# Attention with normalised queries and keys, then a feed-forward block: the first quad's squares split over two engines, and the work at the start of the last stage put in other places

## The chip, the cores and the metric

The kernel runs on one core of a Trainium2 chip. A core has engines with a queue of instructions each: TensorE (PE in the profile; its weight loads are listed as PEld), VectorE (DVE), ScalarE (ACT), GpSimd (POOL) and SyncE (SP), which issues nearly all of the kernel's transfers. An engine works through its queue in order, and waits where an instruction needs something that isn't there yet. The metric is the time of one execution on the device in microseconds (us). It covers a little more than the span, which is the time from the first to the last instruction of the profile.

## The reference

Two parts follow each other. Everything is float32; q, k and v have the shape (8, 12, 448, 64): 8 batches, 12 heads, 448 rows, 64 columns.

```python
q_n, k_n = (rmsnorm(q, g_q), rmsnorm(k, g_k))     # x / sqrt(mean(x * x) + 1e-06) * g
scores = scale * np.matmul(q_n, k_n.transpose(0, 1, 3, 2))
attn = np.exp(scores - max) / (sum + 1e-09)
attn_out = np.matmul(attn, v)
x = attn_out.transpose(0, 2, 1, 3).reshape(3584, 768)

h = x @ w_in                                      # 768 x 1024
e = np.exp(h - h_max)
solu = h * e / (np.sum(e) + 1e-09)
ln = (solu - mean) / np.sqrt(var + 1e-06) * g_ln
out = ln @ w_out                                  # 1024 x 768
```

## The kernel before

The work has three stages, all in the function `fast_path`, and PE goes from one to the next without a barrier.

**Attention.** A "pair" is two heads of one batch; a "quad" `m` is two pairs, `a = 2m` and `b = 2m + 1`. There are 24 quads. The program order of this stage is written out by hand: `tc.manual_schedule()` keeps each engine's instructions in the order in which the Python code issues them. For each pair the rows of q and k are squared (`squares`, one ACT instruction of 128x896, L662), summed over 32 columns (`row_sums`, a DVE reduction, L670), and, for the two pairs of a quad together, the two halves of a head are added by `fold_sums`: four POOL copies of 32 partitions (L680) and an addition (L681). `rsqrt_seed` takes the inverse root by Ln and Exp on ACT (L687, L688), `rsqrt_step` refines it by one Newton step of four small DVE instructions (L694 to L697), `normalise` multiplies q and k by it on POOL (L703), `qk_transpose` is a DVE transpose (L713), and `gain` multiplies by the gains on ACT (L717). Then `scores` multiplies keys by queries on PE in three blocks of keys (L802), `scores_last` does the last 64 keys of both pairs at once (L815), and each block is followed by its exponential E on ACT (L792). `add` adds two blocks of E on DVE (L829), `add_more` a third on POOL (L838), `values` and `values_last` multiply E by v, and `sums` gets the sums of E.

The first quad, m = 0, has a sequence of its own (from L1394), since nothing is ready ahead of it. Pairs 0 and 1 are loaded and normalised in another layout (`square_rows`, `normalise_rows` at L762, `transpose_rows` and `take_rows`), and between their scores the squares of pairs 2 and 3 (quad 1) and 4 and 5 (quad 2) are made, with `fold_sums(1)` and `fold_sums(2)`. The call `norms_next()` stands for the inverse root and the normalisation of the next quad. In this text the "fourth pair" is pair 3.

**The product with w_in.** 3584 tokens are 28 tiles `t` of 128; a group `g` of 14 holds tiles 2g and 2g + 1. A group's product is done in seven partial products (Strassen's scheme, `products`), which end with P4 and P3; the results are added up by DVE (L996), which also keeps the maximum of a row. When a tile's h is complete, `done` plans its five further steps: exponential (`ff_exp`, ACT, L1051), product (`ff_mult`, DVE, L1055), moments (`ff_moments`: two BNStats of 128x512 at L1063, small DVE instructions at L1064 to L1068, then a power and a product on POOL at L1069 and L1071), normalisation (`ff_norm`, ACT, L1075) and `ff_spread`, a DVE transpose (L1084) followed by four stores from SP (L1087) that write the tile to a buffer `ud` in DRAM. The steps are due a number of units after the tile is complete; a unit is one partial product in this stage, and four slots in the last. By default the units are (1, 2, 3, 5, 7); three of the last four tiles have their own (L1096 to L1098). Of a group the tile 2g + 1 is complete first, so tile 26 is the last one.

**The product with w_out.** The last stage has seven supersteps `n` of four tiles each (4n to 4n + 3). Both the four tiles together and each partial product inside are done with Strassen's scheme, seven outer products by seven inner ones. The outer ones run in the order P1, P5, P6, P2, P7, P3, P4, seven slots apart (`STEP`), and the inner ones of an outer product are put in slots 0, 4, 8, 10, 12, 16 and 20 from its start (`PLACES`), so three outer products overlap. A slot is one inner product, four matmuls of 128x192. Its results are copied from the PSUM banks A, B, C by ACT (L1206) or added by DVE (L1208, L1233, L1246, L1256); banks are reused, so a later group of matmuls waits until the reader is done. `both` (L1284) adds two results.

The operands of a superstep are called a11, s1, s2, a12, s3, s4, a22. `load_u` reads tiles from `ud` (SP, L1131); `make` forms the operands: a11, a12 and a22 are ACT copies (L1149, L1151, L1153), s1 is a DVE addition (L1155), s2, s3 and s4 are DVE subtractions (L1157, L1159, L1161), each in two halves `t` of 128x512. s2 is s1 minus a11, s3 is a11 minus a loaded tile, s4 is a12 minus s2. `inner_sums` makes four more sums of each operand on POOL (L1172 to L1175, 128x256 each). In which slot each half is made is set by `made(n, name, slot of half 0, slot of half 1)`; for superstep 0 the slots are its own (L1590 on), for the others they are set against the superstep before. The dictionary `at` maps slots to such calls, and after each slot's matmuls they are issued in order; due steps of `later` come with the matmuls of the slot.

Of the kernel before, what the change touches and what calls it, by code (L numbers as in the profile page):

```python
# [366 lines left out]
def fast_path(  # L367
# [274 lines left out]
    def load_v(m, queue=nc.sync):  # L642
# [13 lines left out]
                lasts[m + i] = vl[:, 2 * i : 2 * i + 2]  # L656
        d["vl"] = lasts.pop(m)

    def squares(n):
        d = st[n]  # L660
        d["sq"] = work.tile([P, 2 * NB, 32], FP32, tag="sq", name="sq", bufs=2)
        nc.scalar.activation(d["sq"].rearrange("p (s b) d -> p s (b d)", s=2), d["qk"], AF.Square)  # L662
# [429 lines left out]
    def in_parts():  # L1092
        def done(g, i):
            t = 2 * g + i
            ff_max(t)
            waits = {  # L1096
                (NG - 2, 1): (1, 2, 3, 5, 5), (NG - 1, 1): (1, 2, 3.25, 6.75, 7), (NG - 1, 0): (2.25, 3.75, 4.75, 7.5, 8)
            }.get((g, i), (1, 2, 3, 5, 7))  # L1098
            for x, f in zip(waits, (ff_exp, ff_mult, ff_moments, ff_norm, ff_spread)):
                later(x, lambda f=f: f(t))  # L1100

        p = [products(g, lambda i, g=g: done(g, i)) for g in range(NG)]
        parts = [p[0][1], p[0][2]]
        for g in range(NG):
            turn = [p[g][6], p[g][5], p[g][7], p[g][4], p[g][3]]
            x = len(parts)
            if g + 1 < NG:
                turn[3:] = [p[g + 1][1], p[g][4], p[g + 1][2], p[g][3]]
            parts += turn
            if g + 1 < NG:  # L1110
                follow(parts, x, lambda g=g: sizes(g + 1))
                follow(parts, x + 1, lambda g=g: block_sums(g + 1, 0))
                follow(parts, x + 2, lambda g=g: block_sums(g + 1, 1))
            if g + 2 < NG:
                follow(parts, x + 4, lambda g=g: load_x(g + 2))
        return parts
# [27 lines left out]
    def make(n, name, t):  # L1144


        o = operand(n, name)[:, t]
        if name == "a11":
            nc.scalar.copy(o, in_turn(n, t, 0))  # L1149
        elif name == "a12":  # L1150
            nc.scalar.copy(o, in_turn(n, t, 1))  # L1151
        elif name == "a22":
            nc.scalar.copy(o, in_turn(n, 2 + t, 1))  # L1153
        elif name == "s1":
            nc.vector.tensor_tensor(o, in_turn(n, 2 + t, 0), in_turn(n, 2 + t, 1), OP.add)  # L1155
        elif name == "s2":
            nc.vector.tensor_tensor(o, us[n, "s1"][:, t], us[n, "a11"][:, t], OP.subtract)  # L1157
        elif name == "s3":
            nc.vector.tensor_tensor(o, us[n, "a11"][:, t], in_turn(n, 2 + t, 0), OP.subtract)  # L1159
        else:  # L1160
            nc.vector.tensor_tensor(o, us[n, "a12"][:, t], us[n, "s2"][:, t], OP.subtract)  # L1161
# [144 lines left out]
    def unit(f, steps=4):  # L1306
        nonlocal now
        f()
        now += steps
        due = [x for x in todo if x[0] <= now]  # L1310
        todo[:] = [x for x in todo if x[0] > now]
        for _, g in sorted(due, key=lambda x: x[0]):
            g()
# [40 lines left out]
    with tc.manual_schedule():  # L1354
# [19 lines left out]
        for m in range(NQ):  # L1374
            a, b = 2 * m, 2 * m + 1

            def outputs():
                values_last(m)
                values(a)


            next1 = m + 1 < NQ
            next2 = m + 2 < NQ
            next3 = m + 3 < NQ
            early = m > 0 and next1

            def norms_next():
                rsqrt_seed(norms[m + 1])
                rsqrt_step(norms[m + 1])
                normalise(a + 2)  # L1390
                normalise(b + 2)

            if m == 0:
                unit(lambda: scores(a, 0))  # L1394
                normalise_rows(1, 0)
                normalise_rows(1, 1)
                unit(lambda: scores(a, 1))
                unit(lambda: scores(a, 2))
                for s in range(2):
                    transpose_rows(1, s)  # L1400
                    take_rows(1, s)
                squares(2)
                add(a)
                add_more(a)
                row_sums(2)
                unit(lambda: scores_last(m))
                squares(3)
                unit(lambda: scores(b, 0))
                row_sums(3)
                fold_sums(1)  # L1410
                unit(lambda: scores(b, 1))
                unit(lambda: scores(b, 2))
                add(b)
                norms_next()
                squares(4)
                row_sums(4)
                squares(5)
                unit(outputs)
                qk_transpose(2)
                gain(2)  # L1420
                row_sums(5)
                qk_transpose(3)
                fold_sums(2)
                unit(lambda: values(b))
                unit(lambda: sums(m))
                inverse(m)
                later(1, lambda m=m: divide(m))
                continue
            if early:
                norms_next()  # L1430
            for x in joins_at.get(m, ()):
                combine_in(x)
            if next1:
                load_v(m + 1)
            if m == 1:
                load(m + 3)
            unit(lambda: scores(a, 0))
            if m == 1:
                gain(3)
            store_x(m - 1)  # L1440
            if early:
                qk_transpose(a + 2)
                if next3 and m > 1:
                    load(m + 3)
            unit(lambda: scores(a, 1))
            unit(lambda: scores(a, 2))
            unit(lambda: scores_last(m))
            unit(lambda: scores(b, 0))
            unit(lambda: scores(b, 1))
            if early:  # L1450
                qk_transpose(b + 2)
            add(a)
            if not on_vector(m):
                add_more(a)
            unit(lambda: scores(b, 2))
            if next2:
                squares(a + 4)
                squares(b + 4)
                row_sums(a + 4)
            if next1:  # L1460
                gain(a + 2)
                gain(b + 2)
            if next2:
                row_sums(b + 4)
                fold_sums(m + 2)
            add(b)
            if on_vector(m):
                add_more(a)
                add_more(b)
            unit(outputs)  # L1470
            step(m - 2)
            begin(m)
            step(m - 1)
            if m - 1 in sets:
                load_next()
            if m == 2:
                load_next()
                load_next()
            if m == 3:
                norm_gain()  # L1480
            unit(lambda: values(b))
            if m == NQ - 1:
                block_sums(0, 0)
                block_sums(0, 1)
                load_x(1)
            unit(lambda: sums(m))
            inverse(m)
            if next1:
                later(1, lambda m=m: divide(m))
            if m == NQ - 2:  # L1490
                load_x(0)
                sizes(0)
# [54 lines left out]
        def when(slot, f):  # L1547
            at.setdefault(slot, []).append(f)
# [6 lines left out]
        for n in range(NS):  # L1555
            base = period * n
            for i, name in enumerate(ORDER):
                q = len(ORDER) * n + i
                for place, f in zip(PLACES, outer_product(n, name, q)):
                    assert STEP * q + place not in slots  # L1560
                    slots[STEP * q + place] = f
                x = HALVES[name][0]
                if q > 1:
                    when(STEP * q - 6, lambda n=n, x=x: inner_sums(n, x))
            for x, t, slot in (("V", 1, 31), ("V", 0, 34), ("C22", 1, 45), ("C22", 0, 52)):
                when(base + slot, lambda n=n, x=x, t=t: both(n, x, t))
            if n == 0:
# [3 lines left out]
            blocks = (0, 0), (1, 0), (2, 0), (3, 0), (2, 1), (3, 1), (0, 1), (1, 1)  # L1571
            for slot, (t, h) in zip(at_load, blocks):
                when(base + slot, lambda n=n, t=t, h=h: load_u(n, t, h))
            late = 6 if n == 1 else 0
            made(n, "a11", base + 12 + late, base + 15 + late)
            made(n, "s1", base + 21 + late, base + 24 + late)
            made(n, "s2", base + 28 + late, base + 38)
            made(n, "a12", base + 33, base + 36)
            made(n, "s3", base + 40, base + 42)
            made(n, "s4", base + 47, base + 49)  # L1580
            made(n, "a22", base + 53, base + 55)

        for h in range(2):
            for t in (2, 3):
# [2 lines left out]
            load_u(0, t, 1)  # L1587
        for x in ("s2", "a12", "s3", "s4", "a22"):
            operand(0, x)
        made(0, "s2", 0, 3)  # L1590
        made(0, "s3", 6, 8)
        made(0, "a12", 10, 11)
        made(0, "a22", 12, 14)
# [87 lines left out]
```

## Time and profile before

| What | us |
|---|---|
| runs of the kernel | 806.71, 807.04, 807.82 (median 807.04) |
| the profiled execution | 807.2 |
| its span | 805.4 |
| span from the start to the second quad's first scores | 26.0 |
| start of the last stage (first group of L1194) | 569.6 |

The granted clock of PE was 0.997 of full speed over the span. Two quantities of the profile have to be kept apart. An engine's busy time is the sum of its instructions; what an engine costs is the time that PE, which is nearly always busy, stands still for it. The profile gives this as the idle time ahead of an instruction, with the name of what it waited for in square brackets. The timeline lists an engine's instructions with start and length; lines with "x4" are four alike in a row. Of POOL's queue one sees at the handover from the second to the last stage that it has a long pause, here 9.41 us:

```profile
576.56 0.86 POOL L1069 TENSOR_TENSOR he<-he,mhalf 128x1 f32<-128x1 f32 x1 [9.41 <-ACT u L1206]
577.52 1.37 POOL L1071 TENSOR_SCALAR shift<-mv,he 128x1 f32<-128x1 f32 x1
578.84 0.73 POOL L1172 TENSOR_TENSOR sums<-s 128x256 f32<-128x256 f32 x1
```

The first start of the second line and the end of the line before show that instructions of one engine follow each other within some tenths of a microsecond if nothing holds them.

### The profile page before, as it was taken

What the parts mean: (1) busy time and instruction counts of PE and PEld (TensorE: products, weight loads), DVE (VectorE), ACT (ScalarE), POOL (GpSimd) and SP (SyncE); (2) the same over time, 40 slices, a digit from 0 to 9 for tenths busy, and PEclk for the clock granted to TensorE, in tenths of its full rate; (3) what the DMA queues carried; (4) which work ended last, traced back from release to release, by engine and by line L of the source; (5) the groups of instructions that cost most, each with busy time, mean ns of one, the idle gap of its engine ahead of it and who ended that gap; (6) DMA issues with size and microseconds to landing.
All of it is one profiled execution on the core that took longest, in us unless ns stands there. A gap on an engine that the chain in (4) does not pass through costs nothing.

```text
span 805.4 us, 14271 instructions
## 1 busy us (share of the span) xinstructions
PE 789.7 (98%) x4854; PEld 464.5 (58%) x4854; DVE 612.8 (76%) x1203; ACT 473.0 (59%) x783; POOL 519.9 (65%) x662
## 2 busy tenths in 40 slices
PE   8999999999999999999999999999899999999997
PEld 4344444443444433444444444444699999999996
DVE  6787989989888896488778667776886776866945
ACT  6677878878778764467767544453505455464420
POOL 2666777778777775244466466678487777777861
PEclk9999999999999999999999999999999999999999
DMA  9878899897787832555545445542647457366312
GB/s 170 159 168 156 182 194 184 196 187 161 165 160 169 161 103 66 140 131 151 150 131 147 102 119 140 141 110 52 210 125 252 133 188 267 117 229 213 120 60 83
DMA packets 269598, 122.68 MB, mean 152 GB/s; under 512 B 187596, under 2 KB 254668, under 8 KB 269516
## 3 DMA queue, kind: packets, MB, share of 16 engines
q1 hardware_dynamic: 254332, 111.78, 55.7%
q10 hardware_dynamic: 15184, 9.90, 4.5%
q8 instruction: 40, 0.66, 0.3%
q14 instruction: 42, 0.34, 0.1%
HBM read 84.94 MB, written 36.70 MB: 151 GB/s over the span
## 4 chain that ended last, share of the span: by engine, by line
PE 88%; DVE 3%; DMA 2%; SPq 2%; POOL 2%; ACT 1%; issue 1%; DVEq 0%; ACTq 0%; POOLq 0%
PE A L1194 15%; PE A L980 13%; PE o L859 12%; PE s L802 12%; PE B L980 8%; PE B L1194 8%; PE C L980 4%; PE sm L881 4%; PE D L980 4%; PE C L1194 4%; PE s L815 2%; PE o L848 2%; SPq L636 1%; DMA ur<-ud 1%; DMA xg<-xd 1%
## 5 line engine op out<-in xcount | busy, mean ns | idle before, releaser
L792 ACT ACTIVATE E<-s 128x896 f32<-128x896 f32 x168 | 138.8, 939 | 8.9 <-PE s L802 8.1
L802 PE MATMUL s<-qkT 64*64 64x448 f32 x1152 | 120.1, 545 | 1.7 <-ACT qkT L717 1.0
L859 PE MATMUL o<-E,v 128*64 128x448 f32 x576 | 113.8, 543 | 0.0
L1069 POOL TENSOR_TENSOR he<-he,mhalf 128x1 f32<-128x1 f32 x28 | 27.6, 986 | 105.6 <-DVE he L1068 95.7
L1194 PE MATMUL B<-w_out,sums 128*128 128x192 f32 x392 | 80.6, 329 | 3.3 <-DVE P L1256 2.1
L802 PEld LDWEIGHTS s<-qkT 64*64 64x64 f32 x1152 | 48.1, 163 | 60.0 <-ACT E L792 29.2
L1194 PE MATMUL A<-w_out,sums 128*128 128x192 f32 x392 | 80.6, 329 | 1.0 <-POOL sums L1175 0.7
L859 PEld LDWEIGHTS o<-E,v 128*64 128x64 f32 x576 | 39.1, 137 | 72.2 <-issue 68.0
L703 POOL TENSOR_TENSOR qkn<-qk,ny 128x896 f32<-128x896 f32 x46 | 77.1, 1697 | 3.5 <-DMA qk<-in_q_dram 1.5
L838 POOL TENSOR_TENSOR es<-es,E 128x896 f32<-128x896 f32 x22 | 46.4, 2109 | 48.9 <-ACT sq L662 35.4
L980 PE MATMUL B<-w_in,xsum 128*128 128x512 f32 x168 | 76.7, 593 | 0.5 <-POOL he L1069 0.5
L980 PE MATMUL A<-w_in,xg 128*128 128x512 f32 x168 | 74.6, 593 | 0.0
L1194 PEld LDWEIGHTS B<-w_out,sums 128*128 128x128 f32 x392 | 66.9, 191 | 3.9 <-DVE P L1256 2.4
L1051 ACT ACTIVATE u<-h,hmax 128x1024 f32<-128x1024 f32 x28 | 32.1, 1148 | 62.7 <-DVE hmax L1045 62.7
L1194 PEld LDWEIGHTS A<-w_out,sums 128*128 128x128 f32 x392 | 66.8, 191 | 1.7 <-POOL sums L1175 1.6
L980 PEld LDWEIGHTS B<-w_in,xsum 128*128 128x128 f32 x168 | 31.8, 190 | 41.0 <-issue 39.0
L980 PEld LDWEIGHTS A<-w_in,xg 128*128 128x128 f32 x168 | 31.8, 190 | 40.1 <-issue 39.3
L829 DVE TENSOR_TENSOR es<-E 128x896 f32<-128x896 f32 x48 | 53.0, 1107 | 2.1 <-ACT E L792 2.1
L670 DVE TENSOR_REDUCE part<-sq 128x28 f32<-128x896 f32 x46 | 47.9, 1080 | 4.4 <-ACT sq L662 2.0
L680 POOL COPY ss<-part 32x56 f32<-32x56 f32 x92 | 46.8, 508 | 6.7 <-DVE part L670 2.2
L713 DVE STREAM_TRANSPOSE qkT<-qkn 128x896 f32<-128x896 f32 x46 | 48.4, 1087 | 0.4 <-POOL qkn L703 0.4
L1194 PE MATMUL A<-w_out,s 128*128 128x192 f32 x224 | 45.6, 326 | 0.0
(150 smaller groups left out, 1647.8 us busy)
## 6 DMA issues: line engine op xcount, KB each, us to landing
ur<-ud SPq DMA_DIRECT2D x60, 256.0 KB, 4.7
ud<-ub SPq DMA_DIRECT2D x112, 128.0 KB, 2.3
xd<-xo SPq DMA_DIRECT2D x48, 224.0 KB, 3.0
qk<-in_q_dram SPq DMA_DIRECT2D x92, 112.0 KB, 3.2
qk<-in_k_dram SPq DMA_DIRECT2D x92, 112.0 KB, 3.0
v<-in_v_dram SPq DMA_DIRECT2D x24, 384.0 KB, 4.4
out_dram<-P SPq DMA_DIRECT2D x19, 384.0 KB, 4.3
raw<-in_moe_w_in_dram SPq DMA_DIRECT2D x12, 512.0 KB, 5.5
```

Of the source, the lines that this page charges most:

```text
L670: nc.vector.tensor_reduce(norms[m]["part"][:, i], st[n]["sq"], AX, OP.add)
L680: e.tensor_copy(ss[g * 32 : g * 32 + 32], part[o * 32 : o * 32 + 32])
L703: e.tensor_tensor(d["qkn"].rearrange("p (s b) d -> p s b d", s=2), d["qk"].rearrange("p s (b d) -> p s b d", d=32), y.rearrange("p (s b) - ...
L713: nc.vector.transpose(d["qkT"].rearrange("p s t -> p (s t)"), d["qkn"].rearrange("p b d -> p (b d)"))
L792: nc.scalar.activation(d["E", kc], s[:, :, 0:S], AF.Exp)
L802: nc.tensor.matmul(s[c : c + D, h, 0:S], d["qkT"][hh, 1, keys], d["qkT"][hh, 0, :], start=True, stop=True,)
L829: nc.vector.tensor_tensor(d["es"], d["E", 0], d["E", 1], OP.add)
L838: e.tensor_tensor(d["es"], d["es"], d["E", 2], OP.add)
L859: nc.tensor.matmul(d["o"][h * D : (h + 1) * D, :], quads[n // 2]["v"][:, n % 2 + 2 * h, kc], d["E", kc][:, h], start=False, stop=(kc == NJ ...
L881: nc.tensor.matmul(sm[g : g + 32, :], ones[:, w], e[:, h, t * S // 2 : (t + 1) * S // 2], start=(x == 0), stop=(x == len(terms) - 1),)
L980: nc.tensor.matmul(k[bank], a[:, c], w_in[i][:, c], start=begin and c == 0, stop=c == HD - 1, skip_group_check=not begin,)
L1194: nc.tensor.matmul(k[bank], a[:, c].rearrange("p a i -> p (a i)"), w_out[:, area, i, c], start=begin and c == 0, stop=c == KC - 1, skip_gr ...
```

## The change

In the first quad, the squares of the fourth pair are made in two halves: q's by DVE, ahead of the second pair's `transpose_rows`, and k's by ACT, behind `squares(2)`. `row_sums(3)` and `fold_sums(1)` come directly after `scores_last`, and the exponential of `scores(b, 2)` is issued behind `norms_next()`'s instructions. PE's order stays the same.

In the second stage the units after which the last tiles' steps are due are changed: tile 24 has its moments and normalisation one unit later; tile 27 its transpose a quarter; tile 26 its product half a unit, its moments two, its normalisation half a unit and its transpose three quarters. On DVE this puts one result of the last w_in group (L996) ahead of tile 24's moments, and tile 26's moments behind several results of the last stage.

In the last stage s2 of superstep 0 is made by POOL in slots 0 and 1 (DVE in slots 0 and 3 before), the inner sums of superstep 0's third outer product (s2) are issued at slot 5 (8 before), and s1, s2, s3, s4 and a22 of superstep 1 are made in later slots, from 39 to 57 (27 to 55 before). The other supersteps keep their slots.

```diff
+    def squares_half(n, s, vector):
+        d = st[n]
+        if s == 0:
+            d["sq"] = work.tile([P, 2 * NB, 32], FP32, tag="sq", name="sq", bufs=2)
+        y, x = d["sq"].rearrange("p (s b) d -> p s (b d)", s=2)[:, s], d["qk"][:, s]
+        if vector:
+            nc.vector.tensor_tensor(y, x, x, OP.mult)
+        else:
+            nc.scalar.activation(y, x, AF.Square)
...
             waits = {
-                (NG - 2, 1): (1, 2, 3, 5, 5), (NG - 1, 1): (1, 2, 3.25, 6.75, 7), (NG - 1, 0): (2.25, 3.75, 4.75, 7.5, 8)
+                (NG - 2, 1): (1, 2, 3, 5, 5), (NG - 2, 0): (1, 2, 4, 6, 7),
+                (NG - 1, 1): (1, 2, 3.25, 6.75, 7.25), (NG - 1, 0): (2.25, 4.25, 6.75, 8, 8.75),
             }.get((g, i), (1, 2, 3, 5, 7))
...
         elif name == "s2":
-            nc.vector.tensor_tensor(o, us[n, "s1"][:, t], us[n, "a11"][:, t], OP.subtract)
+            (nc.vector if n else nc.gpsimd).tensor_tensor(o, us[n, "s1"][:, t], us[n, "a11"][:, t], OP.subtract)
...
                 unit(lambda: scores(a, 2))
+                squares_half(3, 0, True)
                 for s in range(2):
                     transpose_rows(1, s)
                     take_rows(1, s)
                 squares(2)
+                squares_half(3, 1, False)
                 add(a)
                 add_more(a)
                 row_sums(2)
                 unit(lambda: scores_last(m))
-                squares(3)
-                unit(lambda: scores(b, 0))
                 row_sums(3)
                 fold_sums(1)
+                unit(lambda: scores(b, 0))
                 unit(lambda: scores(b, 1))
-                unit(lambda: scores(b, 2))
                 add(b)
                 norms_next()
+                unit(lambda: scores(b, 2))
                 squares(4)
...
                 if q > 1:
-                    when(STEP * q - 6, lambda n=n, x=x: inner_sums(n, x))
+                    when(STEP * q - 6 if q > 2 else 5, lambda n=n, x=x: inner_sums(n, x))
...
-            late = 6 if n == 1 else 0
-            made(n, "a11", base + 12 + late, base + 15 + late)
-            made(n, "s1", base + 21 + late, base + 24 + late)
-            made(n, "s2", base + 28 + late, base + 38)
+            late = n == 1
+            made(n, "a11", base + 12 + 6 * late, base + 15 + 6 * late)
+            made(n, "s1", base + 21 + 18 * late, base + 24 + 17 * late)
+            made(n, "s2", base + 28 + 15 * late, base + 38 + 7 * late)
             made(n, "a12", base + 33, base + 36)
-            made(n, "s3", base + 40, base + 42)
-            made(n, "s4", base + 47, base + 49)
-            made(n, "a22", base + 53, base + 55)
+            made(n, "s3", base + 40 + 7 * late, base + 42 + 7 * late)
+            made(n, "s4", base + 47 + 4 * late, base + 49 + 4 * late)
+            made(n, "a22", base + 53 + 2 * late, base + 55 + 2 * late)
...
-        made(0, "s2", 0, 3)
+        made(0, "s2", 0, 1)
```

## The prediction

> **What bounds the kernel now.** I read the page's busy line first, then the chain that ended last, then the waits of TensorE (PE), and only then the timelines around the two places that the diff touches.
>
> ```profile
> PE 789.7 (98%) x4854; PEld 464.5 (58%) x4854; DVE 612.8 (76%) x1203; ACT 473.0 (59%) x783; POOL 519.9 (65%) x662
> PE 88%; DVE 3%; DMA 2%; SPq 2%; POOL 2%; ACT 1%; issue 1%; DVEq 0%; ACTq 0%; POOLq 0%
> ```
>
> PE is busy for 789.7 of 805.4 us and carries 88% of the chain. The change touches no matmul, so it can win only from PE's 15.7 idle us and from stretches where PE's clock was low. The list of PE's waits says which idle time is large (columns: total, times, longest, us):
>
> ```profile
> PE B L1194 <- DVE P L1256: 2.1, 1, 2.1
> PE s L815 <- ACT E L792: 1.3, 2, 0.7
> PE s L802 <- ACT qkT L717: 1.0, 1, 1.0
> PE B L1194 <- DVE P L1246: 1.2, 1, 1.2
> PE A L1194 <- POOL sums L1175: 0.7, 1, 0.7
> PE B L980 <- POOL he L1069: 0.5, 1, 0.5
> ```
>
> PE's timeline places them; two lie in the second quad, four where the w_in stage hands over to the last stage:
>
> ```profile
> 26.02 2.60 PE L802 MATMUL s<-qkT 64*64 64x448 f32 x24 [1.03 <-ACT qkT L717]
> 29.28 1.53 PE L815 MATMUL s<-qkT 64*64 64x448 f32 x8 [0.66 <-ACT E L792]
> ...
> 566.92 2.81 PE L980 MATMUL B<-w_in,xsum 128*128 128x512 f32 x6 [0.52 <-POOL he L1069]
> ...
> 579.34 0.92 PE L1194 MATMUL B<-w_out,sums 128*128 128x192 f32 x4 [1.16 <-DVE P L1246]
> ...
> 584.35 0.92 PE L1194 MATMUL B<-w_out,sums 128*128 128x192 f32 x4 [2.15 <-DVE P L1256]
> ...
> 586.16 1.49 PE L1194 MATMUL A<-w_out,sums 128*128 128x192 f32 x4
> ...
> 597.47 0.89 PE L1194 MATMUL A<-w_out,sums 128*128 128x192 f32 x4 [0.66 <-POOL sums L1175]
> ```
>
> Start to start, undisturbed groups of four matmuls are 0.65 apart. Against that, 579.34 comes 1.32 late, 584.35 2.31 late, 597.47 0.82 late; 566.92 is 0.69 late against six-matmul groups of 2.58. The windows show why 585.10 to 588.72 took 3.62 us for three groups (1.67 too long): after the long idle time the granted clock (column PEclk) fell.
>
> ```profile
> 579.00:584.00 5.00, 2.87 (x16) 2.57 (x16) 4.83 (x14) 3.54 (x6) 4.58 (x8) 1.00 0.71 250
> 584.00:589.00 5.00, 4.65 (x18) 4.65 (x19) 2.85 (x9) 0.42 (x1) 4.92 (x7) 0.66 0.73 202
> ```
>
> With 0.38 of small change after the stalls, the handover loses 0.69 + 1.32 + 2.31 + 1.67 + 0.82 + 0.38 = 7.2 us. From 579 to 584 DVE is busy 4.83 of 5.00: it is the late engine there, and its timeline shows with what.
>
> ```profile
> 577.53 1.22 DVE L1055 TENSOR_TENSOR u<-h,u 128x1024 f32<-128x1024 f32 x1
> ...
> 578.93 0.35 DVE L1246 TENSOR_TENSOR P<-B,u 128x192 f32<-128x192 f32 x1
> ...
> 579.46 1.28 DVE L1063 BATCH_NORM_STATS2 bs<-u 128x6 f32<-128x512 f32 x2
> ...
> 582.82 1.23 DVE L1084 STREAM_TRANSPOSE ub<-u 128x1024 f32<-128x1024 f32 x1
> 583.98 0.31 DVE L1256 TENSOR_TENSOR P<-B,u 128x192 f32<-128x192 f32 x1
> ```
>
> PE's group at 584.35 needs the 0.31 us sum at 583.98; ahead of it in DVE's queue stand the moments and the transpose of the last token tiles.
>
> **The Trainium skill.** "PSUM — Partial Sum Buffer", section Engine vs sequencer instructions, says that the queues of ScalarE (ACT), VectorE (DVE) and GpSimd (POOL) are strictly first in, first out. The trace agrees: ACT's E at 28.33 stood behind the Ln at 27.80, which waited 1.83 for POOL. "SBUF — State Buffer", section Who interferes with whom, says that a DVE instruction with two SBUF inputs and a GpSimd instruction lock each other out of a shared port, whichever issues second. It agrees: of the four POOL copies from 18.73 (1.83 us together) one ran 1.04 and the others some 0.25, beside DVE's two-input add at 19.11; POOL's shift at 577.52 took 1.37 under DVE's L1055 and 0.26 elsewhere. I use this below.
>
> **First quad.** Removed: the 0.94 us ACT square of the fourth pair. Added: a DVE square of 128x448 and an ACT square of 128x448. Neither shape is in the trace; ACT's 128x896 at 0.94 and its 128x448 copies at 0.65 bound ACT's half between 0.47 and 0.67; DVE's 128x512 two-input ops ran 0.68, so 0.6. DVE's half costs nothing: it fits the 1.03 idle before DVE's copy at 13.93, from about 12.8 to 13.4; were it 0.5 longer, PE's third group of scores would be late by as much. ACT's half pushes E of scores_last from 15.71 to about 15.83, hidden since PE has scores until 17.5. row_sums(3) then ends at 17.55 instead of 18.59, and POOL (free at 17.81) starts the fold at 17.87 instead of 18.73. DVE's add(b), at 18.40, now runs into the third copy, as it did before: I take the end of the fold at 20.1 (19.25 without the collision, 20.22 with the worst) instead of 20.94. Behind it: Ln and Exp, Newton step, normalise, transpose, gain, so scores of the second quad could start by 0.85 earlier; PE is free at 25.0, so the 1.03 wait is nearly gone. But scores(b,2)'s E now stands behind Ln and Exp on ACT, and squares(4) behind it, which costs 0.36 of the lead for the second fold. The wait at 29.28 ends on that chain (fold, Ln, E): it moves from 29.28 to about 28.65. Gain 0.6, bounds 0.2 to 1.5; from there PE runs unbroken and carries the lead on.
>
> **Moments later.** The B sum of the last w_in product now precedes the moments of tile 24 on DVE: PE's group at 566.92 starts at 566.23, gain 0.69 + 0.07. From the new order of DVE's instructions: s2 (1.20 from start to next start) and L1055 of the last tile (1.14) no longer stand ahead of the first L1246, and all before it runs 0.69 earlier: 578.93 − 3.03 = 575.9. The moments of the last tile (579.46 to 581.69, 2.23) and its transpose (1.16) no longer stand ahead of L1256: 583.98 − 3.03 − 3.39 = 577.6 by the queue alone; the L1161 ahead of it waits for s2, a12 and its own turn, and its bank for PE, so I take 579.75. PE wants it at about 580.4. The waits of 1.32 and 2.31 go, with the low clock behind them. What comes later instead: norm and transpose of tiles 27 and 26. SP's order stays as it was: tile 27's four stores stand ahead of the last two loads of superstep 1, which feed its a12 at slots 33 and 36; tile 26's stand ahead of output stores alone, and superstep 6 is the first to read them. Both are hidden; if tile 27's transpose came 3 us later than the old 582.82, a12 would be what PE waits for.
>
> **s2 on POOL.** Two DVE subtractions of 128x512 (1.28 together, at 571.77) leave DVE. On POOL, 128x256 ran 0.73 and 128x384 1.00, so 1.27 each by extension; the first ends at about 570, the second at 572.4 with L1055 blocking it once. PE needs the first half's product at 573.4: hidden by 1 us. POOL was idle for 9.41 there, so nothing else is late, except that inner_sums of s2 and a12 now go ahead of the last pow and shift; that is hidden by the later norm.
>
> **What is late next.** Two new waits. ACT's u3 copy (L1206) is queued behind a12 copies that wait for a load landing at 573.6: PE stops for 0.54 at 574.7. And P6's P7 group at about 581.7 waits 0.65 to 0.95 for a bank read by L1246, because ACT's a11 copies wait for a landing at about 578.6. I take 0.54 + 0.75.
>
> **Operands of n=1 later.** Eight DVE pieces now stand in slots 39 to 53: 14 slots of 0.65 are 9.1 us of PE. In the old trace the eight ran 0.97, 1.10, 1.21, 0.68, 0.68, 0.69, 0.68, 0.95: 7.0 us. In the same stretch DVE has 14 sums of 0.35 and three L1284 of 0.55 to 1.1: 7.1 us. Less 0.075 overlap for each of 25, 12.2 us against 9.1: DVE falls 3 us behind, of which the slack of the product order covers most; I charge 0.8 (0 to 2.5). The old wait at 597.47 (0.82) goes, because POOL's sums no longer meet two-input DVE work there.
>
> **Sum.** 7.2 − 0.54 − 0.75 − 0.8 = 5.1 in the handover and 0.6 in the first quads: 5.7, of which I keep 5.6. The profiled execution took 807.2 (span 805.4 plus 1.8 around it), so 801.6, span 799.8; the median of the runs is 807.04, 0.16 lower, so **801.4**.
>
> **Rivals.**
> 1. *Fuller gain.* The loads land early enough, the fold escapes the collision, DVE's lag is absorbed: 7.2 + 0.6 to 1.5, so 798.3 to 799.2, and up to 800.3 if one of the three stays. For it: from 589 to 597.5 PE lost only the 0.82 although DVE was busy 8.43 of 8.50. Against: the loads stand in SP's queue behind the stores of tiles 25 and 24, which come little earlier.
> 2. *The wait changes place.* The stall at 584.35 goes, but ACT's queue and the landings stop PE for over 1.5 us in one place, 0.7 more than I charge, so that the clock falls again (1.67): 5.6 − 0.7 − 1.67 = 3.2, so 803.8. For it: both new waits come from ACT's queue behind a DMA. Against: 0.54 and 0.75 are short beside the idle time that brought the clock down.
> 3. *Slower: DVE overload in the n=1 stretch.* If all eight pieces run at the dearest rate seen (1.21, beside POOL's sums), 9.7 + 7.1 = 16.8 us stand against 9.1, and if the product order gives no slack, all of the lag of 7.7 stops PE. The rest of the gain is 5.6 + 0.8 = 6.4: 1.3 slower, 808.3. It decides from a lag of 6.4 that reaches PE. Against: half of the pieces ran 0.68.
> 4. *The first quad doesn't do what it says.* The collision of add(b) and the fold keeps the fold's end at 20.9 and squares(4) is later: gain 0 to −0.4, total 4.9, 802.1.
>
> **How the numbers follow.** Chances: forecast (800.3 to 802.8, own range) with rival 4 inside it 0.55, of which rival 4 is 0.12; rival 1 0.13; rival 2 0.22 (802.8 to 806); rival 3 0.10, some of it short of 807. Leaving out the ends of rivals 1 and 2 and all of rival 3, the range is 799.0 to 805.0. About 0.2% (1.6 us) is what can be told from no change: faster 0.87, within it 0.04, slower 0.09.
>
> **What would show it.** In the new profile: PE's scores at about 25.4 and the last-key scores near 28.65; no wait on L1256 over 1 us and PEclk 1.00 in the slice after the handover; POOL's subtraction twice at about 1.27; small new waits at A or B groups, on ACT u or DVE P, near 574 and 582; and DVE near full from slot 39 of the last stage, with PE waits on L1256 under 1 us. I am wrong if a wait of over 2 us on DVE P or on a late landing stands in the first two supersteps, or if the second fold ends later than 27.8.

## The result

The changed kernel took 803.39 us (median of 5 runs, 802.33 to 803.57), the kernel before 806.71 in 5 runs (805.98 to 807.82). The ratio is 0.9952 with a 95% interval of 0.9941 to 0.9963, that is 3.9 us (3.0 to 4.8) faster; the medians are 3.3 apart. The forecast was 801.4, 5.6 faster. The span of the profiled execution fell from 805.4 to 801.6.

Line numbers of the changed kernel's lines are 10 higher up to `in_parts` and 11 higher in most of the last stage: L802 exponential, L1085 normalisation, L1094 transpose, L1168 s2, L1257 and L1267 the sums out of bank B. In other variants they shift by as much as their edits.

PE's waits in the changed kernel (total, times, longest, us):

```profile
PE s L825 <- ACT E L802: 1.7, 2, 1.0
PE A L1205 <- POOL sums L1185: 1.2, 1, 1.2
PE A L1205 <- DVE u L1219: 0.6, 2, 0.4
PE B L1205 <- DVE P L1267: 0.5, 1, 0.5
PE s L812 <- ACT qkT L727: 0.4, 1, 0.4
PE A L1205 <- ACT u L1217: 0.2, 1, 0.2
```

The waits of 2.1, 1.2, 0.7 and 0.5 on DVE and POOL at the handover are gone, the one of 1.0 on qkT is down to 0.4. New are one of 1.2, which the profile puts down to POOL's sums (it is DVE's, as shown below), and several of 0.2 to 0.5; and the wait on E, 1.3 before, has grown to 1.7. PE's timeline says where:

```profile
25.51 2.60 PE L812 MATMUL s<-qkT 64*64 64x448 f32 x24 [0.40 <-ACT qkT L727]
...
306.21 0.98 PE L825 MATMUL s<-qkT 64*64 64x448 f32 x8 [1.01 <-ACT E L802]
...
566.14 2.74 PE L990 MATMUL B<-w_in,xsum 128*128 128x512 f32 x6
...
575.15 0.92 PE L1205 MATMUL A<-w_out,a 128*128 128x192 f32 x4 [0.22 <-ACT u L1217]
...
577.85 0.81 PE L1205 MATMUL B<-w_out,sums 128*128 128x192 f32 x4
...
580.61 0.82 PE L1205 MATMUL B<-w_out,sums 128*128 128x192 f32 x4
...
583.30 0.89 PE L1205 MATMUL A<-w_out,sums 128*128 128x192 f32 x4 [1.22 <-POOL sums L1185]
...
600.90 0.92 PE L1205 MATMUL B<-w_out,sums 128*128 128x192 f32 x4 [0.46 <-DVE P L1267]
...
605.31 0.92 PE L1205 MATMUL A<-w_out,a 128*128 128x192 f32 x4 [0.24 <-DVE u L1219]
```

PE's order is the same in both kernels, so the same group of matmuls can be looked up in both traces, and the difference of its two starts (after minus before) is the lead won so far; a minus sign says that the group starts earlier. Where the difference makes a step, time was won or lost. Worked out from the two traces:

| group, start before | step, us | what |
|---|---|---|
| to 26.02 | +0.12, then −0.63 | start of the program; scores of the second quad |
| 306.30 | +0.43 | last quad: the lead is down to 0.08 |
| 566.92 | −0.76 | last w_in product |
| 575.42 | +0.49 | new: ACT's copy u3 |
| 579.34 and 584.35 | −1.42, −2.41 | the two waits on DVE |
| 585 to 589 | −1.67 | PE's low clock: three groups took 3.62 us before, and 1.95 is usual |
| 586.16 | +1.45 | new: the wait at 583.30 |
| 597.47 | −0.90 | the wait put down to POOL's sums |
| 605.34 and 609.24 | +0.73, +0.51 | new: DVE in superstep 1's late slots |

A step includes what the groups after a stall or a start are longer by, about 0.1 us. Three smaller steps in the last stage make +0.2 together; the sum is −3.83. In what follows "lead" is always this difference against the trace of the kernel before, and the "handover" is the part of it from 560 us on: −3.74 for the changed kernel.

DVE is no longer late for the two sums out of bank B, L1257 at 576.41 (578.93 before) and L1267 at 580.11 (583.98 before), and the transpose stands behind them:

```profile
576.41 0.35 DVE L1257 TENSOR_TENSOR P<-B,u 128x192 f32<-128x192 f32 x1
...
579.84 0.36 DVE L1257 TENSOR_TENSOR P<-B,u 128x192 f32<-128x192 f32 x1 [0.27 <-ACT u L1217]
580.11 0.35 DVE L1267 TENSOR_TENSOR P<-B,u 128x192 f32<-128x192 f32 x1
580.38 1.23 DVE L1094 STREAM_TRANSPOSE ub<-u 128x1024 f32<-128x1024 f32 x1
```

For the new wait at 583.30 the profile names POOL's sums. POOL's timeline in the changed kernel:

```profile
568.07 2.52 POOL L1168 TENSOR_TENSOR s<-s,a 128x512 f32<-128x512 f32 x2
575.17 0.87 POOL L1079 TENSOR_TENSOR he<-he,mhalf 128x1 f32<-128x1 f32 x1 [4.59 <-ACT u L1217]
576.13 0.27 POOL L1081 TENSOR_SCALAR shift<-mv,he 128x1 f32<-128x1 f32 x1
576.36 0.73 POOL L1183 TENSOR_TENSOR sums<-s 128x256 f32<-128x256 f32 x1
577.17 1.59 POOL L1184 TENSOR_TENSOR sums<-sums,s 128x256 f32<-128x256 f32 x1
...
582.03 1.17 POOL L1185 TENSOR_TENSOR sums<-a 128x256 f32<-128x256 f32 x1
```

s2 is done at 570.6, but its sums start at 576.36, since tile 24's power and shift stand ahead of them: 4.59 us of idle time in a queue with work. (The power reads what DVE's moments end with, at 575.03; ACT's copy, which the bracket names, ended at about the same time.) The sums of a12 come last, at 580.5 to 583.9.

But PE's group at 583.30 doesn't read the sums of a12. It is the inner P7 of the outer product P6, in slot 26. It reads a sum of s2, and those are done at 580.6; and it adds to a bank A that DVE's sum u (L1219) has to read first. That sum ended at 583.15:

```profile
581.54 1.08 DVE L1172 TENSOR_TENSOR s<-a,s 128x512 f32<-128x512 f32 x1
...
582.81 0.34 DVE L1219 TENSOR_TENSOR u<-A,P 128x192 f32<-128x192 f32 x1
```

In the profiles of all ten kernels with the new due times PE starts this group 0.14 to 0.15 us after DVE's sum ends. Where POOL is named, the instruction is not always the same: the third sum of a12 here, the second with the old slots, the fourth with `sizes` late. With the old slots PE starts at 582.91, when the third sum has only begun:

```profile
582.91 0.89 PE L1205 MATMUL A<-w_out,sums 128*128 128x192 f32 x4 [0.78 <-POOL sums L1184]
```

```profile
582.78 0.73 POOL L1185 TENSOR_TENSOR sums<-a 128x256 f32<-128x256 f32 x1
```

So this is a wait on DVE, where the transpose of 580.38 and half of s4 (L1172) stand ahead of the sum. The wait of 0.66 at 597.47 in the kernel before has the same form (inner P7 of P7, slot 40): DVE's sum u ended 0.15 ahead of PE's start, behind a piece of s2 of 1.21, and the POOL sums named are of an operand that this group doesn't read.

### The profile page after: what moved, and what is told of

Its sections match the earlier page's. It is cut to its first block, busy times and chain, and to the rows that moved or that the text cites. A ratio compares the mean times of both kernels' runs of the same rounds, so it can differ in the third digit from the quotient of the medians.

```text
span 801.6 us, 14271 instructions
## 1 busy us (share of the span) xinstructions
PE 788.1 (98%) x4854; PEld 462.7 (58%) x4854; DVE 613.7 (77%) x1202; ACT 472.2 (59%) x783; POOL 523.1 (65%) x664
## 4 chain that ended last, share of the span: by engine, by line
PE 87%; DVE 3%; DMA 2%; SPq 2%; POOL 2%; ACT 2%; issue 1%; DVEq 0%; ACTq 0%; POOLq 0%
PE A L1205 14%; PE A L990 13%; PE o L869 12%; PE s L812 12%; PE B L990 8%; PE B L1205 7%; PE C L990 4%; PE sm L891 4%; PE D L990 4%; PE C L1205 3%; PE s L825 2%; PE o L858 2%; SPq L636 1%; DMA xg<-xd 1%; ACT E L802 1%
## 5 line engine op out<-in xcount | busy, mean ns | idle before, releaser
L802 ACT ACTIVATE E<-s 128x896 f32<-128x896 f32 x168 | 138.8, 937 | 8.3 <-PE s L812 7.8
L563 POOL TENSOR_TENSOR w_out<-w_out 128x384 f32<-128x384 f32 x44 | 45.0, 1028 | 1.3
```

The lines of the kernel that those rows point to most:

```text
L563: nc.gpsimd.tensor_tensor(o, p, q, OP.subtract)
L802: nc.scalar.activation(d["E", kc], s[:, :, 0:S], AF.Exp)
```

## Experiments

Each kernel was run in turns with the kernel before on the same chip; the ratio is against that. Two columns of the table come from the one profiled execution of each: the lead after the last quad and the handover.

| kernel | median us | ratio (95%) | lead at 309 | handover |
|---|---|---|---|---|
| changed | 803.39 | 0.9952 (0.9941 to 0.9963) | −0.08 | −3.74 |
| first quad alone | 806.99 | 0.9998 (0.9989 to 1.0007) | +0.58 | −1.04 |
| late slots alone | 805.96 | 0.9989 (0.9980 to 0.9997) | +0.30 | −0.21 |
| due times alone | 804.96 | 0.9979 (0.9971 to 0.9987) | +1.14 | −2.51 |
| changed, old due times | 805.16 | 0.9978 (0.9967 to 0.9988) | +0.14 | −2.93 |
| changed, old slots | 803.93 | 0.9962 (0.9950 to 0.9974) | +0.33 | −3.53 |
| changed, s2 on DVE | 803.17 | 0.9948 (0.9931 to 0.9964) | −0.04 | −3.95 |
| changed, sizes late | 802.10 | 0.9939 (0.9924 to 0.9955) | −1.29 | −3.09 |
| changed, sums early | 802.88 | 0.9955 (0.9940 to 0.9970) | −0.49 | −4.34 |
| both moves | 801.82 | 0.9943 (0.9929 to 0.9957) | −1.63 | −3.95 |
| and a11 behind u3 | 801.54 | 0.9935 (0.9920 to 0.9950) | −1.16 | −4.55 |
| and transpose later | 802.24 | 0.9949 (0.9936 to 0.9963) | −1.61 | −4.12 |
| and operands spread | 801.00 | 0.9929 (0.9914 to 0.9944) | −1.02 | −5.09 |

Half of a ratio's interval is 0.6 to 1.3 us, so a step of half a microsecond can be seen in the traces only; and as a trace is one execution, such a step can be chance. The +0.49 at ACT's copy u3 is an example. It stands in the changed kernel's trace alone: in the nine other kernels with the new due times the group starts without a wait. The copies ahead of u3 in ACT's queue wait for a load; the first of them starts 4.85 us after the last stage's first group in the changed kernel's trace, and 3.7 to 4.5 us after it in the nine.

### The first quad alone

The kernel before with the diff's lines in the first quad and nothing else.

> The kernel before with the first quad's edit alone. Theory: the second quad's first scores start 0.5 to 0.6 us earlier, PE keeps that lead until the last quad, and loses it there, because ACT's sizes of the first w_in group (the Square with a row sum, ahead of that quad's exponentials) wait for a load whose landing does not follow the lead: shift at the end of the span 0.0 to -0.2, time 0 to 0.2 us below before. Rival: the load's landing varies by chance and the lead reaches the end: 0.5 to 0.6 us below before.

The lead is 0.61 at 303 us (0.50 in the changed kernel), and then it turns into a loss of 0.58. The time is the same as before within 0.1%. PE's group and ACT's instruction behind it in this kernel:

```profile
306.87 0.98 PE L825 MATMUL s<-qkT 64*64 64x448 f32 x8 [1.79 <-ACT E L802]
```

```profile
304.12 0.84 ACT L951 ACTIVATE xsum<-xg 128x768 f32<-128x768 f32 x1 [5.84 <-DMA xg<-xd]
```

The second fence is ACT's timeline: `sizes` stands ahead of the last quad's exponentials, and waits 5.84 us for the load of the first w_in group. In the nine traces with this order the load was issued at 296.2 to 296.4 where the first quad is new and at 296.9 to 297.0 where it is old; ACT went on behind it at 304.12, 303.45, 303.88, 303.50, 303.68 and 303.05 with the new, and at 303.54, 303.83 and 304.68 with the old. The means differ by 0.4, but single values scatter by 1.6. So the lead of 0.6 isn't cut off exactly, as the theory had it; PE waits for a landing that scatters by more than the lead. How much of it gets through on average these runs leave open. The handover of −1.04, in a kernel that doesn't touch it, is taken up below.

### The three other parts

Due times alone is the kernel before with the two new lines in `waits`; late slots alone the kernel before with the block from `late = n == 1` to a22. The other three undo one part of the changed kernel:

```diff
-            (nc.vector if n else nc.gpsimd).tensor_tensor(o, us[n, "s1"][:, t], us[n, "a11"][:, t], OP.subtract)
+            nc.vector.tensor_tensor(o, us[n, "s1"][:, t], us[n, "a11"][:, t], OP.subtract)
...
-                    when(STEP * q - 6 if q > 2 else 5, lambda n=n, x=x: inner_sums(n, x))
+                    when(STEP * q - 6, lambda n=n, x=x: inner_sums(n, x))
...
-        made(0, "s2", 0, 1)
+        made(0, "s2", 0, 3)
```

(that is s2 on DVE; old due times and old slots put the lines of before back).

> The changed kernel with the old due times of the last tiles' steps. Theory: this is the part that pays: the last tile's moments and transpose stand ahead of DVE's sums out of bank B again, the wait on L1267 of about 1.5 to 2.3 us and the 0.5 to 0.7 us at the last w_in product come back, with a low clock behind the long one: 2.5 to 4.5 us above the changed kernel. Rival: s2 on POOL and the later slots already clear DVE there, and the old due times cost only the 0.7 us at the last w_in product: 0.5 to 1 us above the changed kernel.

> The changed kernel with superstep 0's s2 on DVE again (slots 0 and 3) and its sums at slot 8. Theory: 1.28 us more ahead of DVE's sums out of bank B; the first of them has about 1.4 us to spare and the next about 0.3, so PE stops for 0.7 to 1.2 us near 580.6, and the POOL sums come no later: 0.5 to 1.5 us above the changed kernel. Rival: s2 on POOL is what takes POOL's port from DVE's L1065 (1.88 instead of 1.22), and giving it back to DVE costs nothing: within 0.3 us of the changed kernel.

> The changed kernel with superstep 1's operands in their old slots (s1 27 and 30, s2 34 and 38, s3 40 and 42, s4 47 and 49, a22 53 and 55). Theory: the late slots only exchange one wait for others: the two stalls behind DVE at 600.9 and 605.3 (0.55 + 0.51) go and POOL's sums make one of 0.8 to 0.9 near 592.5; time within 0.5 us of the changed kernel. Rival: with the moments and transposes of tiles 27 and 26 now late, the old slots put s1 and s2 in the same stretch of DVE (583 to 590), and PE loses 1.5 to 3 us there: 805 to 806.5.

With the old due times the time rises by 2.1 us (ratio 0.9978 against 0.9952), and in the trace the last w_in product is 0.67 later and the wait on L1267 is back at 1.53. DVE's timeline there has the moments and the transpose ahead of the sum again:

```profile
578.39 1.27 DVE L1073 BATCH_NORM_STATS2 bs<-u 128x6 f32<-128x512 f32 x2
...
581.74 1.23 DVE L1094 STREAM_TRANSPOSE ub<-u 128x1024 f32<-128x1024 f32 x1
582.90 0.31 DVE L1266 TENSOR_TENSOR P<-B,u 128x192 f32<-128x192 f32 x1
```

The theory named the place; its price of 2.5 to 4.5 us wasn't reached. In this trace the wait was shorter than the old 2.15 and no low clock followed. The runs may be dearer than the trace for the clock: over the whole run it was 0.997 or less in 7 of their 11, and in none of the changed kernel's 5.

With s2 on DVE nothing is lost: ratio 0.9948, handover 0.2 better, and DVE's L1065 takes 1.22 us in place of 1.88, as the rival says. There is a wait of 0.43 at 579.4, on POOL's second sum of s2. The later one, at slot 26, is 0.78 in place of 1.22; but so it is with the old slots, where s2 stays on POOL. The rival holds: neither the runs nor the trace show that s2 on POOL is worth anything in the changed kernel.

With the old slots the kernel is at 0.9962. The theory said an even exchange, the rival 1.5 to 3 us; from slot 27 on, where this edit begins, the trace has a loss of 0.86 + 1.03 + 0.28, of which 0.64 + 0.51 come back where the late slots stall:

```profile
591.00 0.92 PE L1205 MATMUL A<-w_out,a 128*128 128x192 f32 x4 [0.59 <-DVE u L1219]
...
594.00 0.89 PE L1205 MATMUL A<-w_out,sums 128*128 128x192 f32 x4 [0.78 <-POOL sums L1183]
```

(The second is again an inner P7, and DVE's sum u ended 0.15 ahead of it.) So the late slots are worth 1.0 us in that stretch of this trace, half-way between both. The two handovers differ by 0.2 only, since ahead of slot 27 this trace doesn't have the wait for u3 and has 0.43 less at slot 26, neither of which the edit touches; and the runs, 0.9962 against 0.9952, don't tell the two kernels apart. Are the late slots worth it by themselves?

> The kernel before with superstep 1's late slots alone. Theory: the late slots are worth 1.1 us in the changed kernel because DVE still has tile 26's moments and transpose in that stretch; in the kernel before DVE has caught up by then, so they take away the 0.82 at 597.47 and bring the two stalls of 0.5: within 0.5 us of before. Rival: they are worth their 1.1 us anywhere: 1 to 1.3 us below before.

The trace has the exchange that the theory named: 0.89 won at 597.47, 0.80 lost at 605.34; the handover is −0.21, and the end 0.09 later than before, as 0.29 had been lost by the last quad. The runs say 0.9 us faster (0.2 to 1.6), a little less than the rival's 1.0 to 1.3 but more than the trace, which is of one of the longest of its executions (807.62, median 805.96); the size remains uncertain.

> The kernel before with the new due times of the last tiles' steps alone (first quad, s2 and superstep 1's slots as before). Theory: this is the part that pays. It takes away the 0.7 at the last w_in product and most of the two waits of 1.32 and 2.31 with the low clock behind them (1.67); s2 on DVE keeps one wait of 0.4 to 0.8, and superstep 1's old slots bring 1.1 (seen when they alone were put back): 3.0 to 4.2 us below before, near 803. Rival: undoing it in the changed kernel cost only 1.8 us, so it is worth about that here too, and the rest needs s2 on POOL or the late slots beside it: 1.5 to 2.2 us below before, near 805.

The rival holds: 1.7 us faster (1.0 to 2.3). The trace says where the rest went. The 0.76, 1.42 and 2.41 us of the table above are won, with the 1.67 of the low clock, but PE has four new waits. The first is on POOL's second sum of s2, which ends at 580.51. The others are on DVE, with superstep 1's operands in their old slots behind tile 26's moments; at 584.29 and 596.04 the groups are inner P7 again, and DVE's sum u ended 0.15 ahead of each:

```profile
580.57 0.92 PE L1195 MATMUL A<-w_out,sums 128*128 128x192 f32 x4 [0.42 <-POOL sums L1174]
584.29 0.89 PE L1195 MATMUL A<-w_out,sums 128*128 128x192 f32 x4 [0.78 <-POOL sums L1174]
592.45 0.92 PE L1195 MATMUL A<-w_out,a 128*128 128x192 f32 x4 [0.59 <-DVE u L1209]
596.04 0.89 PE L1195 MATMUL A<-w_out,sums 128*128 128x192 f32 x4 [1.37 <-POOL sums L1174]
```

Due times and late slots belong together: the first move DVE's work out of the handover, the second clear the stretch that it moves into.

### The waits that are left

Two edits on the changed kernel, first alone and then together: `sizes(0)` behind the last quad's exponentials, and the sums of s2 at slot 2.

```diff
                 load_x(0)
-                sizes(0)
...
             if m == NQ - 1:
+                sizes(0)
                 block_sums(0, 0)
...
-                    when(STEP * q - 6 if q > 2 else 5, lambda n=n, x=x: inner_sums(n, x))
+                    when(STEP * q - 6 if q > 2 else 2, lambda n=n, x=x: inner_sums(n, x))
```

> The changed kernel with ACT's sizes of the first w_in group issued behind the last quad's seven exponentials instead of ahead of them. Theory: the wait of PE at 306.2 (1.0 us in the changed kernel, for an exponential queued behind a load) goes, POOL's block sums end about 5 us later, at 318, and PE needs the first of them at 320.5: the first quad's lead of 0.6 now reaches the end, and the 0.6 of the kernel before with it: shift of 1.0 to 1.1 us against the changed kernel, 802.3. Rival: POOL's block sums become what PE waits for near 320, or another wait takes its place: less than 0.3 us.

PE's wait in the last quad is gone, and the lead there is 1.29:

```profile
305.26 0.93 PE L825 MATMUL s<-qkT 64*64 64x448 f32 x8
```

POOL's block sums end at 316, and PE takes them without a wait. This shows that the wait was the queue behind the load. Of the 1.2 us won, only 0.56 reach the end of this trace: at the handover PE stops for 0.79 at 579.30, for ACT's copy u3 behind a load's landing. By the ratios, 0.9939 against 0.9952, the runs are 1.0 us below the changed kernel, with intervals that overlap.

> The changed kernel with the inner sums of superstep 0's s2 issued at slot 2, ahead of tile 24's power and shift in POOL's queue. Theory: the wait of 1.22 us at 583.3 is POOL's own order: its sums stood behind a power that waits 4.6 us for DVE. The four sums fit into that pause, those of a12 end 2.7 us earlier, the wait goes: 1.2 to 1.4 us below the changed kernel, 802.1. Rival: DVE's two-input work slows the sums wherever they stand, or DVE's sums out of the banks are as late as POOL: 0 to 0.5 us.

POOL's order was the cause of its late sums, as the theory says: the four sums of s2 now lie in the pause.

```profile
570.23 1.59 POOL L1183 TENSOR_TENSOR sums<-s 128x256 f32<-128x256 f32 x1
...
573.28 0.74 POOL L1186 TENSOR_TENSOR sums<-s,sums 128x256 f32<-128x256 f32 x1
574.74 0.86 POOL L1079 TENSOR_TENSOR he<-he,mhalf 128x1 f32<-128x1 f32 x1 [0.72 <-ACT a L1164]
```

But only 0.44 is won at the group of 583.30, and the profile now names DVE:

```profile
582.32 0.89 PE L1205 MATMUL A<-w_out,sums 128*128 128x192 f32 x4 [0.78 <-DVE u L1219]
```

The rival holds. PE waited for DVE's sum in the changed kernel too, as shown above, so POOL's order was not the cause of the wait. What was won is in DVE's queue: half of s4 (L1172), ahead of that sum, took 1.08 us beside a POOL sum of 1.17, and takes 0.65 here, with POOL's sums over at 580.15. With the old slots it took 0.64 without an edit at that place, and there POOL's sum was the longer one, 1.07 in place of 0.73. The runs, 0.9955 against 0.9952, show no gain.

> The changed kernel with both: sizes behind the exponentials, sums of s2 at slot 2. If both theories hold, the gains add, since 260 us of unbroken PE lie between them: 2.2 to 2.5 us below the changed kernel, about 801.0. If the rivals hold, 0 to 0.8.

The trace's lead against the changed kernel is 1.76 (of which 0.50 is the wait for u3 that this trace doesn't have), the medians are 1.6 apart, and the ratios 0.7, with intervals that overlap: between the theories in the trace, as the second edit gives less. What is left was taken in turn, with superstep 1's a11 one slot later (`base + 12 + 7 * late, base + 15 + 7 * late`), then with tile 27's transpose at 7.75 in place of 7.25, then with s1, s2, s3 and s4 of superstep 1 in slots 37 to 57.

> The kernel with both moves, and superstep 1's a11 one slot later (19 and 22), so that ACT's copy of u3 stands ahead of a copy that waits for a load. Theory: what is left near 578.6 (0.64 us in the kernel with both moves) is ACT's queue: u3's matmuls end at 575.97, its copy runs at 578.19, when the load ahead of it has landed; with the new order this wait is under 0.1. DVE's sums behind it come 0.5 us earlier, but the wait on DVE at 581.6 (0.78) stays, so about 0.5 of the 0.75 is kept: 801.3. Rival: the landing sets the place anyway, through a11's own readers: 0 to 0.1 us.

ACT's timeline, first with both moves, then with a11 behind u3:

```profile
577.67 0.62 ACT L1160 COPY a<-ur 128x512 f32<-128x512 f32 x1 [1.56 <-DMA ur<-ud]
578.19 0.31 ACT L1217 COPY u<-A 128x192 f32<-128x192 f32 x1
```

```profile
576.50 0.31 ACT L1217 COPY u<-A 128x192 f32<-128x192 f32 x1
578.12 0.62 ACT L1160 COPY a<-ur 128x512 f32<-128x512 f32 x1 [1.31 <-DMA ur<-ud]
```

The copy no longer waits for a landing that it doesn't need; PE's 0.64 is gone, the handover 0.60 better. The theory holds in the trace, and the wait on DVE stays at 0.78.

> The same, and tile 27's transpose half a unit later, behind two DVE sums out of bank A. Theory: PE's wait of 0.78 at 581.6 is DVE's queue, where the 1.23 us transpose stands ahead of the sum that PE needs; behind it it hides, since its stores are needed far later: 1.3 to 1.5 us below the kernel with both moves, 800.4. Rival: the transpose delays the moments of tile 26 and the next sums by as much: 0.5 us, as without it.

The 0.78 is down to 0.08, which shows that DVE's queue made this wait; and 0.62 comes four groups later, on another of DVE's sums, now behind the transpose:

```profile
583.72 0.92 PE L1205 MATMUL A<-w_out,s 128*128 128x192 f32 x4 [0.62 <-DVE u L1219]
```

The rival holds, and the runs show no gain. Neither of the two places tried for the transpose is free for PE.

> The same, and superstep 1's DVE operands spread over slots 37 to 57 in place of 39 to 53 (s1 37 and 40, s2 42 and 44, s3 47 and 50, s4 54 and 57). Theory: the stalls at 600.9 and 605.3 (0.55 + 0.51 with their restarts) come from eight pieces in 14 slots; over 20 slots DVE keeps up: 0.7 to 1.1 us below the kernel before this, 799.6. Rival: the stalls come from single pieces of 0.95 to 1.2 us beside POOL's sums right ahead of a sum that PE needs, wherever they stand: within 0.3 us.

Of the stalls on L1267 and L1219 near 600 us 0.12 and nothing are left, and the handover is 0.97 better, as the theory says. This is the fastest kernel of the study, 801.00 us, 0.9929 of the kernel before; its interval overlaps those of the kernels near it.

## Why the prediction was right, and which terms were off

The direction, the place and the range held; the gain was put 1.7 to 2.3 us too high. The 803.39 is inside the range because that had room for the rivals: it lies outside the forecast's own 800.3 to 802.8. By its own steps:

**First quad.** The chain is as forecast: row sums, fold with the collision (end of the fold 20.3, forecast 20.1), second quad's scores 0.63 earlier (0.62), the last-key scores at 28.77 (28.65). The step that failed is "from there PE runs unbroken and carries the lead on": the lead was 0.50 until the last quad and 0.08 after it. The page shown before had this wait in its list, as one of the two on E L792; the forecast used the first, at 29.28, and overlooked the second, 0.61 us at 306.30.

**What goes at the handover.** Forecast 7.2 in all. The steps measured 0.76 + 1.42 + 2.41 + 1.67 + 0.90 = 7.16, so in the trace this came true. But the 1.67 of the low clock was taken as certain from the one execution profiled, and it isn't in each of them (last section). The reason given for the 0.82 at 597.47, two-input DVE work beside POOL's sums, fits, except that PE waits there for DVE and not for the sums.

**What comes.** Forecast 0.54 + 0.75 + 0.8 = 2.1; measured 0.49 + 1.45 + 1.24 = 3.2, and 0.2 in small steps. These terms were too small. The first is right in cause and size in this trace; but it is in none of the nine other kernels with the new due times, so that the agreement is luck. The second names the right group, P6's P7 at slot 26, and the right engine. The reader is another, DVE's sum u out of bank A (L1208) and not L1246; and ahead of it stand the transpose and half of s4 rather than ACT's landing: with ACT's copy moved the wait stayed at 0.78, with the transpose moved it fell to 0.08. The half of s4 took 1.08 beside POOL's sum, which makes 1.22 of 0.78; that slowing is one the prediction knew of and didn't count here. The third was an estimate from DVE's load, and 0.44 low.

**s2 on POOL** was costed at nothing, rightly; that it also gives nothing beside the new due times wasn't said.

**The rivals.** The time lies where "the wait changes place" had it (803.8), and a part of that mechanism is there: ACT's queue behind a DMA at 575, and DVE in another place at 583.30. But no wait was above 1.5 and the clock did not fall again; a wait of 1.53 with the old due times left it at 1.00 in its trace. The slower case didn't come near: DVE lost 1.24 us in superstep 1's stretch where 6.4 would have been needed. DVE's pieces there ran 0.68 to 1.21, as taken.

## What to carry to other kernels

Check the name that a profile gives a wait against what the instruction reads and which bank it writes: here POOL's sums of another operand were named, and a sum of DVE's, which ended 0.15 us ahead of PE in each trace, was what PE waited for. A step of half a microsecond between two traces can be a load that landed late in one of them; look for it in the traces of the neighbouring kernels. A lead that is won early has to pass every later wait on a transfer; go through PE's whole list of waits and not only the largest, and move work that waits for a transfer behind work that doesn't in each queue. Work that is put off lands in a stretch with its own load, so that moving it and making room for it are one change.

## What was not expected of the hardware

The low clock after the long stall isn't there every time. PE's windows from 585 to 589 us, in the kernel before and in the kernel with the first quad alone, which has the same two stalls of 1.16 and 2.15 us (columns: window, length, busy time of PE, PEld, DVE, ACT and POOL with instructions, granted clock, DMA share, GB/s):

```profile
585.00:589.00 4.00, 4.00 (x16) 4.00 (x15) 1.85 (x7) 0.00 (x0) 3.92 (x6) 0.57 0.90 249
```

```profile
585.00:589.00 4.00, 4.00 (x24) 3.79 (x25) 3.25 (x8) 0.00 (x0) 3.92 (x6) 1.00 0.79 212
```

16 matmuls at a clock of 0.57 against 24 at 1.00. It is worth 1.67 us in the kernel before, and most of that is still there in the handover of −1.04 of a kernel without an edit at that place. It makes the term of 1.67 in the table above a matter of the execution: the comparison of the two profiles holds it in full, the runs in part. How large a part can be estimated from the clock that each run has on record, a mean over the whole run. Of 78 runs of the kernel before, taken beside the experiments, 36 had 0.997 or less and took 807.7 us on average, 42 had 0.998 or more and took 806.5. If that difference is the low clock at this place, as it is in the runs profiled, it makes about 0.6 us on average. Of the 57 runs of the ten kernels with the new due times 5 had 0.997 or less. The Trainium skill, "TensorE: Matmul & The Clock Gate", section Part 1: The HAM clock gate, has the clock fall to half after an idle window of about 3.4 us, and says that the window runs freely, so that the same kernel differs between runs. In 1 us windows the trace shows 0.50 from 586 to 588, which agrees with the half; but the idle times ahead of it, 1.16 and 2.15 us, were both shorter than 3.4, and no run here shows the window itself.

A subtraction of 128x512 on POOL took 1.26 us (2.52 for two), as extended from the smaller shapes (1.27). Sums of 128x256 that take 0.73 alone took 1.59 with a two-input DVE product at the same time.
